# Attention into a two-layer feed-forward on one core: the last product of the attention as column tiles

## The chip, the cores and the metric

One core of one Trainium2 chip runs the whole program. The metric is the device time of one execution in microseconds, as a median of several runs. The engines are named as in the profile: PE (matrix product), PEld (its weight loads), DVE, ACT, POOL, and SP, which issues the transfers.

## What is computed

Four batches of eight heads, 576 positions, 64 numbers per head. The attention has no softmax: both `q` and `k` go through a feature map of 256 features, and the sums over the positions are taken before `q` comes in.

```python
def phi(x):
    proj = np.einsum('bhsd,df->bhsf', x, w_phi)
    proj = proj - np.max(np.abs(proj), axis=-1, keepdims=True)
    return np.concatenate([np.exp(proj), np.exp(-proj)], axis=-1)
q_p, k_p = (phi(q), phi(k))
kv = np.einsum('bhsf,bhsd->bhfd', k_p, v)
z = np.sum(k_p, axis=2)
num = np.einsum('bhsf,bhfd->bhsd', q_p, kv)
den = np.einsum('bhsf,bhf->bhs', q_p, z)[..., None] + 1e-06
x = num / den
```

The result, as 2304 tokens of 512 numbers, goes through `g = h * cos(h)`, `h = x @ w_in`, `g @ w_out` and then through a second layer with the square of the positive part in place of `h * cos(h)`. Both layers have 2048 hidden numbers.

## The kernel before

The attention works in 16 units; a unit `u` is two heads of one batch. Its steps carry short names. `PJk`, `PJq`, `PJt` (lines 512 and 521) are the projections on PE: two heads lie in the two row halves of the array. `R...` takes the maximum and subtracts it on DVE, `E...` and `QE...` are the exponentials on ACT, `Q...` (lines 574 and 571) are transposes on PE, `V0`, `V1`, `Vt` (lines 546 and 554) build `kv` and, in a 65th column, `z` in a bank of PSUM.

The steps that the change touches come last. `KS` and `KZ` (lines 564 and 566, DVE) copy `kv` of both heads into `ks`, four blocks of 64 columns: numerators of head 0, the column `z` of head 0 sixty-four times, `z` of head 1 sixty-four times, numerators of head 1. `N` (line 593) multiplies: for one head and one half of the positions (288 columns), two matmuls, one for each half of the 256 features, each with a weight of 128 columns, 64 of numerators and 64 that all give the denominator. There are four such steps per unit, `N00`, `N10`, `N01`, `N11`, each into a PSUM bank of its own, of which there are two. `C` (line 601, ACT) copies each to `tm`. `D1` (SP) brings the 576 denominators of each head from one partition into `cp`, 32 partitions of 36; `I` (DVE) adds 1e-6 and inverts; `D3` writes them to DRAM, `D4` reads them back, spread over 64 partitions per head, and `Z0`, `Z1` (line 631, POOL) multiply, one head each, into `xbuf`, from which the feed-forward reads.

Data is 32-bit float. A 32-bit float matmul of the program is two PE instructions in the trace, with a weight load for each; a transpose, and a matmul of the feed-forward (declared float32r), is one.

The order on each engine is fixed ahead: the tables `STEPS`, `W_STEPS` and `F_STEPS` give each step an engine, a planned cost and a place, and `arrange` lists the steps as they can start by those costs. Between the steps of the units stand the preparation of the feed-forward's weights (`wload`, `wa` to `lo`, on SP, ACT, DVE and POOL) and the first four blocks of the feed-forward. After that the feed-forward follows in a plain loop, three matmuls for each product (lines 289 to 291 and 385).

Of the kernel before, what the change touches and what calls it, by code (L numbers as in the profile page):

```python
# [8 lines left out]
F32 = mybir.dt.float32  # L9
# [24 lines left out]
    "PJk": ("PE", 1.2, -0.0861),  # L34
    "PJq": ("PE", 1.0, -1000.0),
    "PJt": ("PE", 0.5, -0.531),
    "Rk0": ("DVE", 1.39, -0.7547),
    "Rk1": ("DVE", 1.39, -0.587),
    "Rq0": ("DVE", 1.39, 0.0807),
    "Rq1": ("DVE", 1.39, 1.743),  # L40
    "Rt": ("DVE", 0.86, -0.2191),
    "Ek0": ("ACT", 1.12, -2.3061),
    "Ek1": ("ACT", 1.12, -0.6222),
    "Et": ("ACT", 0.52, 0.2442),
    "V0": ("PE", 1.8, -0.4006),
    "V1": ("PE", 1.8, 0.3704),
    "Vt": ("PE", 0.46, 0.8122),
    "KS": ("DVE", 0.44, 0.23),
    "KZ": ("DVE", 0.44, -0.9258),
    "Q0": ("PE", 0.45, 0.6667),  # L50
    "Q1": ("PE", 0.45, 0.8333),
    "Qt": ("PE", 0.12, -1.179),
    "QE0": ("ACT", 1.1, 0.5433),
    "QE1": ("ACT", 1.1, 0.8521),
    "QEt": ("ACT", 0.5, -1.2755),
    "N00": ("PE", 0.98, 1.1469),
    "N10": ("PE", 0.98, 1.4122),
    "N01": ("PE", 0.98, 0.8229),
    "N11": ("PE", 0.98, 1.4454),
    "C00": ("ACT", 0.42, 0.8958),  # L60
    "C10": ("ACT", 0.42, 1.1975),
    "C01": ("ACT", 0.42, 0.8069),
    "C11": ("ACT", 0.42, 2.6994),
    "D1": ("SP", 0.75, 1.3),
    "I": ("DVE", 1.2, 1.7326),
    "D3": ("SP", 0.32, 1.5),
    "D4": ("SP", 1.1, 1.6),
    "Z0": ("POOL", 1.5, 1.9905),
    "Z1": ("POOL", 1.5, 0.312),
# [5 lines left out]
    "wa": ("ACT", 0.58, 15.5),  # L75
    "wb": ("ACT", 0.58, -0.631),
    "wc": ("ACT", 0.58, 0.629),
    "j0": ("DVE", 0.75, -8.494),
    "j1": ("DVE", 1.0, 6.091),
    "add": ("POOL", 1.32, 29.772),  # L80
    "mul": ("POOL", 1.32, -17.661),
    "hi": ("ACT", 0.56, 14.013),
    "lo": ("POOL", 1.32, 41.761),
# [4 lines left out]
    "xh": ("ACT", 0.56, 23.758),  # L88
    "xl": ("DVE", 0.69, 3.914),
    "G1": ("PE", 2.73, 8.892),  # L90
    "A1": ("ACT", 1.05, -24.304),
    "A2a": ("DVE", 0.7, -3.676),
    "A2b": ("DVE", 0.9, 41.064),
    "B1": ("ACT", 1.15, 36.696),
    "B2": ("DVE", 0.7, -14.68),
    "B3": ("ACT", 0.55, 23.9),
    "B4": ("DVE", 0.69, 22.441),
# [61 lines left out]
def attention_ffn_kernel(  # L159
# [27 lines left out]
    with tc.manual_schedule():  # L187
# [281 lines left out]
        with ExitStack() as actx:  # L469
# [31 lines left out]
            def rows(h):  # L501
                return slice(D * h, D * (h + 1))
# [56 lines left out]
            def KS(u, part):  # L559

                kv = kv_t[u]
# [25 lines left out]
            SH = S // 2  # L587

            def N(u, h, half):
# [8 lines left out]
            def C(u, h, half):  # L598
                if h == half == 0:
                    tm_t[u] = late("tm", [P, 2, S])  # L600
                nc.scalar.activation(
                    out=tm_t[u][:, h, half * SH:(half + 1) * SH], in_=nm_t.pop((u, h, half))[:, 0:SH], func=ACTF.Copy
                )
# [14 lines left out]
            def D3(u):  # L618
                db = db_t[u] = dp.tile([2, S], F32, tag="db", name="db", bufs=2)
                nc.sync.dma_start(out=db.rearrange("h (a b) -> (h a) b", a=NI), in_=cp_t.pop(u))  # L620
# [7 lines left out]
            def Z(u, h):  # L628
                b, hp = UNITS[u]
                r = rows(h)  # L630
# [15 lines left out]
            for u in range(NU):  # L646
# [18 lines left out]
                st("KS", (KS, u, 0), ("Vt",), [("ks",)], [("kv",)])  # L665
                st("KZ", (KS, u, 1), ("Vt", "KS"), (), [("kv",), ("ks",)])
# [6 lines left out]
                before = ()  # L673
                for half in range(2):
                    for h in range(2):
                        n, tiles = f"{h}{half}", [("nm", h, half)]
# [7 lines left out]
                for h in range(2):  # L684
                    st(f"Z{h}", (Z, u, h), ("D4",), (), [("tm",), ("dn",)])
# [120 lines left out]
```

## Time and profile before

| | us |
|---|---|
| median of 3 runs | 988.17 (988.00 to 988.29) |
| the profiled execution | 988.67 |
| its span, first to last instruction | 986.9 |
| PE busy within the span | 977.4 (99%) |
| last product, line 593, PE busy | 70.9, 256 instructions |
| same, its weight loads on PEld | 45.1 |
| copies of line 601 on ACT | 25.1, 64 instructions |
| multiplications of line 631 on POOL | 45.6, 32 instructions |

The attention takes the first 190 us or so of the span, the rest is the feed-forward. A busy PE row is not the time that a matmul costs: a matmul's shown length includes the way through the array, so the next one starts well before it ends. The chain of work that ended last shows for each piece the time until the next piece starts, and so what the piece costs.

### The profile page before, as it was taken

The page shows a single profiled execution, that of the slowest core. Times are in us where ns is not written, and L with a number is a line of the kernel's source. Part 1 is how long each engine was busy: PE and PEld are TensorE (multiplying, and loading weights), DVE is VectorE, ACT ScalarE, POOL GpSimd, SP SyncE. Part 2 cuts the span into 40 slices and gives each one's busy share as a digit, 9 for nine tenths or more (in the row PEclk, how much of TensorE's full clock was granted, in tenths as well). Part 3 has the DMA queues.
Part 4 walks back from the last instruction along what each step waited for, and adds up shares of the span by engine and source line. Part 5 has one row for each costly group of instructions (what it writes and reads, how often), then busy time and mean ns, then how long its engine had stood idle before and what let it go on. Part 6 is the DMA issues. An engine that isn't in the chain of part 4 may idle for free.

```text
span 986.9 us, 14043 instructions
## 1 busy us (share of the span) xinstructions
PE 977.4 (99%) x5305; PEld 831.9 (84%) x5305; DVE 548.8 (56%) x944; ACT 625.6 (63%) x1213; POOL 123.3 (12%) x98
## 2 busy tenths in 40 slices
PE   9999999999999999999999999999999999999998
PEld 8988899888889888888888888888888888888897
DVE  5788887789966655565458888983112111211211
ACT  5888888698967665575559879995333433433343
POOL 1577686501000000000000000000000000000000
PEclk9999999999999999999999999999999999999999
DMA  6566532152000000000036660001000000100010
GB/s 228 182 201 225 190 114 88 38 192 77 1 1 2 1 1 1 1 0 1 1 90 193 196 192 12 1 1 44 1 1 17 27 1 1 43 1 1 1 44 22
DMA packets 23284, 60.01 MB, mean 61 GB/s; under 512 B 4400, under 2 KB 4528, under 8 KB 23216
## 3 DMA queue, kind: packets, MB, share of 16 engines
q1 hardware_dynamic: 23072, 59.04, 18.4%
q8 instruction: 42, 0.69, 0.3%
q14 instruction: 26, 0.21, 0.1%
q10 hardware_dynamic: 144, 0.07, 0.0%
HBM read 54.23 MB, written 4.79 MB: 60 GB/s over the span
## 4 chain that ended last, share of the span: by engine, by line
PE 85%; DVE 5%; ACT 4%; DMA 2%; issue 2%; POOL 1%; SPq 0%; DVEq 0%; POOLq 0%
PE acc L385 36%; PE h L291 12%; PE h L290 12%; PE h L289 12%; PE nm L593 4%; PE kv L546 4%; PE pj L512 2%; PE tp L574 1%; DVE tr L311 1%; DMA db<-cp 1%; DMA dn<-db 1%; ACT tr L305 1%; DVE w L259 1%; ACT tr L304 1%; DVE mag L246 1%
## 5 line engine op out<-in xcount | busy, mean ns | idle before, releaser
L327 DVE TENSOR_TENSOR g<-tr,g 128x512 fp32r<-128x512 f32 (+1 forms) x160 | 101.8, 636 | 275.0 <-ACT g L324 274.0
L289 PE MATMUL h<-xs,w 128*128 128x512 f32 (+1 forms) x640 | 235.8, 369 | 0.0
L291 PE MATMUL h<-xs,w 128*128 128x512 f32 (+1 forms) x640 | 235.5, 368 | 0.0
L290 PE MATMUL h<-xs,w 128*128 128x512 f32 (+1 forms) x640 | 235.4, 368 | 0.0
L385 PE MATMUL acc<-g,w 128*128 128x512 f32 (+1 forms) x960 | 208.4, 368 | 0.8 <-DVE g L327 0.8
L385 PE MATMUL acc<-w,g 128*128 128x512 f32 x864 | 206.8, 389 | 0.0
L385 PEld LDWEIGHTS acc<-g,w 128*128 128x128 f32 x960 | 168.1, 189 | 31.5 <-DVE g L327 1.7
L385 PEld LDWEIGHTS acc<-w,g 128*128 128x128 f32 x864 | 161.4, 188 | 32.9
L324 ACT ACTIVATE g<-tr 128x512 fp32r<-128x512 f32 (+1 forms) x160 | 93.8, 586 | 128.0 <-PE acc L385 94.5
L289 PEld LDWEIGHTS h<-xs,w 128*128 128x128 f32 x640 | 120.7, 189 | 20.6
L290 PEld LDWEIGHTS h<-xs,w 128*128 128x128 f32 x640 | 120.6, 188 | 20.5
L291 PEld LDWEIGHTS h<-xs,w 128*128 128x128 f32 x640 | 120.7, 189 | 20.0
L307 ACT ACTIVATE tr<-h 128x512 f32<-128x512 f32 (+1 forms) x80 | 44.2, 552 | 103.8 <-PE h L291 102.7
L309 DVE SCALAR_TENSOR_TENSOR tr<-tr,h 128x512 f32<-128x512 f32 (+1 forms) x80 | 50.7, 634 | 63.1 <-ACT tr L305 61.8
L319 DVE SCALAR_TENSOR_TENSOR tr<-tr,h 128x512 f32<-128x512 f32 (+1 forms) x80 | 50.6, 633 | 40.4 <-ACT tr L315 39.8
L593 PE MATMUL nm<-eq,ks 128*128 128x288 f32 x256 | 70.9, 410 | 0.4 <-DVE ks L566 0.4
L314 ACT ACTIVATE tr<-tr 128x512 f32<-128x512 f32 (+1 forms) x80 | 46.8, 585 | 26.7 <-DVE tr L311 26.7
L304 ACT ACTIVATE tr<-h 128x512 f32<-128x512 f32 (+1 forms) x80 | 43.6, 545 | 30.0 <-PE h L291 29.7
L546 PEld LDWEIGHTS kv<-v,e 128*128 128x128 f32 x512 | 59.8, 192 | 1.7
L546 PE MATMUL kv<-v,e 128*128 128x65 f32 x512 | 59.0, 273 | 0.0
L527 DVE TENSOR_REDUCE m<-pj 128x4 f32<-128x512 f32 (+1 forms) x80 | 49.4, 617 | 8.2 <-PE pj L512 8.2
L631 POOL TENSOR_TENSOR xbuf<-tm,dn 64x576 f32<-64x576 f32 x32 | 45.6, 1426 | 62.4 <-DMA dn<-db 61.2
(55 smaller groups left out, 1052.5 us busy)
## 6 DMA issues: line engine op xcount, KB each, us to landing
raw<-in_dram SPq DMA_DIRECT2D x64, 512.0 KB, 4.3
kq<-in_dram SPq DMA_DIRECT2D x16, 384.0 KB, 3.4
v<-in_dram SPq DMA_DIRECT2D x16, 330.0 KB, 4.3
dn<-db SPq DMA_DIRECT2D x32, 144.0 KB, 3.1
out_dram<-ot SPq DMA_DIRECT2D x18, 256.0 KB, 3.1
kq<-in_dram SPq DMA_DIRECT2D x16, 256.0 KB, 3.5
cp<-tm SPq DMA_DIRECT2D x32, 2.2 KB, 2.4
db<-cp SPq DMA_DIRECT2D x16, 4.5 KB, 3.8
```

The lines of the kernel that those rows point to most:

```text
L289: nc.tensor.matmul(out=hps, lhsT=ih[:, kk, :], rhs=xh, start=kk == 0, stop=False)
L290: nc.tensor.matmul(out=hps, lhsT=ih[:, kk, :], rhs=xl, start=False, stop=False)
L291: nc.tensor.matmul(out=hps, lhsT=il[:, kk, :], rhs=xh, start=False, stop=kk == KDM - 1)
L304: nc.scalar.activation(out=t, in_=h_t[c], func=ACTF.Copy, scale=INV_2PI, bias=ROUND)
L309: nc.vector.scalar_tensor_tensor(out=r, in0=t, scalar=-C1, in1=h_t[c], op0=ALU.mult, op1=ALU.add)
L319: nc.vector.scalar_tensor_tensor(out=t, in0=r, scalar=1.0, in1=h_t.pop(c), op0=ALU.subtract, op1=ALU.mult, reverse0=True)
L324: nc.scalar.activation(out=g[:, 0], in_=t, func=ACTF.Copy)
L327: nc.vector.tensor_tensor(out=g[:, 1], in0=t, in1=f(g[:, 0]), op=ALU.subtract)
L385: nc.tensor.matmul(out=o, lhsT=l, rhs=r, start=c == 0 and i == 0, stop=c == KFF - 1 and i == 2)
L527: nc.vector.tensor_reduce(out=m[:, 0:n], in_=pj[:, 0:n, :], axis=AX.X, op=ALU.max, apply_absolute_value=True)
L546: nc.tensor.matmul(out=acc[:, s, h, 0:D + 1], lhsT=e[:, t, s, :], rhs=v_t[u][:, t, h, 0:D + 1], start=t == 0 and h == 0 and s == 0, stop=F ...
L593: nc.tensor.matmul(out=nm[:, 0:SH], lhsT=ks_t[u][:, s, 2 * h:2 * h + 2, :].rearrange("p a d -> p (a d)"), rhs=eq_t[u][:, h, s, half * SH:( ...
```

## The change

`ks` now has only numerators and one column `z` for each head, and is copied in one instruction. `N` is one step for a unit. It takes both PSUM banks, one for each half of the positions. First come eight matmuls of 288 columns with weights of 64 columns: head 0 writes partitions 0 to 63 of the bank, head 1 partitions 64 to 127 (tiles of 128 rows by 64 columns of the array). Then sixteen matmuls of 144 columns, whose weight is one column `z` thirty-two times: each of four strips of 32 partitions takes one head and one quarter of the positions (tiles of 128 by 32), into columns 288 to 431 of the same bank. `C` copies 432 columns, twice a unit. `D1` reads four partitions, 32 apart, for each half; `D3` is two transfers; `Z` is one multiplication over 128 partitions. All places in the tables are new, so the order on the engines is too; the planned costs change only for the steps touched (`N` 3.5, `C` 0.5, `D3` 0.75).

```diff
-    "N00": ("PE", 0.98, 1.1469),
...
-    "C00": ("ACT", 0.42, 0.8958),
...
+    "N": ("PE", 3.5, 1.6213),
+    "C0": ("ACT", 0.5, 0.9339),
+    "C1": ("ACT", 0.5, 0.1895),
...
-                if part == 0:
-                    ks = ks_t[u] = own("ks", [P, 2, 4, D])
-                    nc.vector.tensor_copy(ks[:, :, 0:4:3, :], kv[:, :, :, 0:D])
-                else:
-                    nc.vector.tensor_copy(ks_t[u][:, :, 1:3, :], kv[:, :, :, D:D + 1].to_broadcast([P, 2, 2, D]))
+                ks = ks_t[u] = own("ks", [P, 2, 2, D + 2])
+                nc.vector.tensor_copy(ks[:, :, :, 0:D + 1], kv_t.pop(u)[:, :, :, 0:D + 1])
...
-                nm = nm_t[u, h, half] = bank("nm")
-                for s in range(2):
-                    nc.tensor.matmul(
-                        out=nm[:, 0:SH], lhsT=ks_t[u][:, s, 2 * h:2 * h + 2, :].rearrange("p a d -> p (a d)"),
-                        rhs=eq_t[u][:, h, s, half * SH:(half + 1) * SH], start=s == 0, stop=s == 1,
-                    )
+                for half in range(2):
+                    nm_t[u, half] = bank("nm")
+                for half in range(2):
+                    for s in range(2):
+                        for h in range(2):
+                            nc.tensor.matmul(
+                                out=nm_t[u, half][rows(h), 0:SH], lhsT=ks[:, s, h, 0:D], rhs=eq[:, h, s, half * SH:(half + 1) * SH],
+                                start=s == 0, stop=s == 1,
+                            )
+                for half in range(2):
+                    for s in range(2):
+                        for i in range(4):
+                            h, o = i // 2, half * SH + (i % 2) * SQ
+                            nc.tensor.matmul(
+                                out=nm_t[u, half][32 * i:32 * i + 32, SH:SH + SQ], lhsT=ks[:, s, h, D:D + 1].to_broadcast([P, 32]),
+                                rhs=eq[:, h, s, o:o + SQ], start=s == 0, stop=s == 1, skip_group_check=True,
+                            )
...
-                for h in range(2):
-                    nc.sync.dma_start(out=cp[h * NI:(h + 1) * NI, :], in_=tm_t[u][D - D * h:D - D * h + 1, h, :])
+                for half in range(2):
+                    nc.sync.dma_start(out=cp[half * NI:(half + 1) * NI, :], in_=tm_t[u][0:P:32, half, SH:SH + SQ])
...
-                nc.sync.dma_start(out=db.rearrange("h (a b) -> (h a) b", a=NI), in_=cp_t.pop(u))
+                for half in range(2):
+                    nc.sync.dma_start(out=db[:, half * SH:(half + 1) * SH], in_=cp[half * NI:(half + 1) * NI, :])
...
-                    out=xbuf[r, hp, b * S:(b + 1) * S], in0=tm_t[u][r, h, :], in1=dn_t[u][r, :], op=ALU.mult
+                    out=xbuf[:, hp, b * S:(b + 1) * S].rearrange("p (a n) -> p a n", a=2), in0=tm_t.pop(u)[:, :, 0:SH],
+                    in1=dn_t.pop(u).rearrange("p (a n) -> p a n", a=2), op=ALU.mult,
...
+                st("N", (N, u), ("KS", "QE0", "QE1", "QEt"), [("nm", 0), ("nm", 1)], [("ks",), ("eq",)])
+                st("C0", (C, u, 0), ("N",), [("tm",)], [("nm", 0)])
+                st("C1", (C, u, 1), ("N", "C0"), (), [("nm", 1)])
```

The order on PE through one unit in the middle of the attention, before (`nm` is the last product, `kv` the sums, `tp` transposes, `pj` projections; the `x` at the end counts matmuls of the program):

```order
L593 MATMUL nm<-eq,ks 128x288 x2
L546 MATMUL kv<-v,e 128x65 x16
L593 MATMUL nm<-eq,ks 128x288 x4
L574 MATMUL tp<-ident,pq 128x128 x4
L554 MATMUL kv<-v,et 128x2x65 x2
L512 MATMUL pj<-wph,kq 128x128 x8
L512 MATMUL pj<-wph,kq_1137 128x128 x8
L574 MATMUL tp<-ident,pq 128x128 x4
L593 MATMUL nm<-eq,ks 128x288 x2
L521 MATMUL pj<-wph,kq_1137 128x128 x2
L571 MATMUL tp<-ident,pt 128x128
```

And the same engine through one unit of the changed kernel:

```order
L562 MATMUL tp<-ident,pq 128x128 x4
L585 MATMUL nm<-eq,ks 64x288 x8
L593 MATMUL nm<-eq,ks 32x144 x16
L539 MATMUL kv<-v,e 128x65 x8
L562 MATMUL tp<-ident,pq 128x128 x4
L514 MATMUL pj<-wph,kq_1452 128x128 x2
L539 MATMUL kv<-v,e 128x65 x8
L559 MATMUL tp<-ident,pt 128x128
L505 MATMUL pj<-wph,kq 128x128 x8
L505 MATMUL pj<-wph,kq_1548 128x128 x8
L547 MATMUL kv<-v,et 128x2x65 x2
```

The four pieces of the last product are now one block of two kinds of tiles, between a transpose and the next unit's `kv`; the two projections and the `kv` sums are otherwise the same work.

On SP, which issues the transfers, one unit in the middle of the attention before (`cp`, `db` and `dn` carry the denominators, `raw` is a feed-forward weight, `kq` and `v` are a unit's inputs):

```order
L620 DMA db<-cp 32x36
L625 DMA dn<-db 64x576 x2
L219 DMA raw<-in_dram 128x1024
L611 DMA cp<-tm 16x1x36 x2
L219 DMA raw<-in_dram 128x1024
L487 DMA kq<-in_dram 128x512
L488 DMA kq_1137<-in_dram 128x768
L489 DMA v<-in_dram 128x660
```

And in the changed kernel:

```order
L620 DMA db<-cp 2x8x36 x2
L625 DMA dn<-db 64x576 x2
L212 DMA raw<-in_dram 128x1024
L609 DMA cp<-tm 16x1x36 x2
L480 DMA kq<-in_dram 128x512
L481 DMA kq_1238<-in_dram 128x768
L482 DMA v<-in_dram 128x660
L212 DMA raw<-in_dram 128x1024
```

What moved there is little: the write of `db` is two transfers, still directly ahead of the read of `dn`.

## Rows read from the trace of the kernel before

**Rows 1.** The page: busy time of each engine; the clock by slices.
```profile
PE 977.4 (99%) x5305; PEld 831.9 (84%) x5305; DVE 548.8 (56%) x944; ACT 625.6 (63%) x1213; POOL 123.3 (12%) x98
PEclk9999999999999999999999999999999999999999
```

**Rows 2.** Stretches: length, busy us (instructions) per engine, clock, DMA share, GB/s.
```profile
0.00:20.00 20.00, 17.71 (x151) 15.77 (x151) 12.61 (x22) 9.13 (x19) 0.70 (x6) 1.00 0.64 215
...
40.00:60.00 20.00, 18.68 (x148) 16.61 (x147) 16.15 (x29) 16.91 (x40) 15.43 (x12) 1.00 0.72 232
...
80.00:100.00 20.00, 19.82 (x167) 17.15 (x167) 16.56 (x29) 17.77 (x39) 16.07 (x13) 1.00 0.65 211
...
120.00:140.00 20.00, 20.00 (x169) 18.07 (x166) 17.30 (x31) 17.73 (x40) 16.42 (x13) 1.00 0.41 125
...
260.00:987.00 727.00, 722.28 (x3453) 608.77 (x3452) 340.66 (x581) 414.70 (x770) 0.00 (x0) 1.00 0.10 30
```

**Rows 3.** Chain that ended last, one unit: start, us to next piece, what.
```profile
100.13 0.97 PE nm L593 x4
101.10 3.52 PE kv L546 x32
104.62 2.00 PE nm L593 x8
106.61 0.44 PE tp L574 x4
107.05 0.45 PE kv L554 x4
107.50 1.99 PE pj L512 x32
109.48 0.59 PE tp L574 x4
110.07 0.97 PE nm L593 x4
111.04 0.44 PE pj L521 x4
111.48 0.11 PE tp L571
111.59 0.97 PE nm L593 x4
```

**Rows 4.** The same chain earlier, where it leaves PE.
```profile
30.69 4.94 DMA db<-cp
...
36.20 3.48 DMA dn<-db
...
41.30 1.42 POOL xbuf L631
...
53.44 0.97 PE nm L593 x4
...
60.98 3.61 DMA raw<-in_dram
...
88.66 0.97 PE nm L593 x4
```

**Rows 5.** Timeline: start, us, eight weight loads and eight matmuls of line 593.
```profile
104.40 1.76 PEld L593 LDWEIGHTS nm<-eq,ks 128*128 128x128 f32 x8
104.45 2.16 PE L593 MATMUL nm<-eq,ks 128*128 128x288 f32 x8
```

**Rows 6.** Groups by line and shape: busy us, mean ns of one | idle before.
```profile
L601 ACT ACTIVATE tm<-nm 128x288 f32<-128x288 f32 x64 | 25.1, 416 | 12.0 <-PE nm L593 7.8 <-POOL xbuf L631 3.3 <-issue 0.6
L585 ACT ACTIVATE eq<-tp 128x512 f32<-128x512 f32 x64 | 34.7, 595 | 17.4 <-PE tp L574 17.0
L566 DVE COPY ks<-kv 128x256 f32<-128x256 f32 x16 | 6.6, 412 | 0.0
L631 POOL TENSOR_TENSOR xbuf<-tm,dn 64x576 f32<-64x576 f32 x32 | 45.6, 1426 | 62.4 <-DMA dn<-db 61.2
L249 POOL TENSOR_TENSOR mag<-mag,raw 128x512 f32<-128x512 f32 x20 | 26.3, 1313 | 1.6
```

More of the change, by code (lines that the diff above doesn't have):

```diff
@@ L33 @@
     "load": ("SP", 1.5, -1.2),
[L34 removed]
+    "PJk": ("PE", 1.2, -0.956),
     "PJq": ("PE", 1.0, -1000.0),
[L36 to L55, printed above, removed]
[L56 to L63 removed]
+    "PJt": ("PE", 0.5, 0.1833),
+    "Rk0": ("DVE", 1.39, -1.2383),
+    "Rk1": ("DVE", 1.39, -0.0484),
+    "Rq0": ("DVE", 1.39, 0.4179),
+    "Rq1": ("DVE", 1.39, 0.7208),
+    "Rt": ("DVE", 0.86, 0.2315),
+    "Ek0": ("ACT", 1.12, 0.6024),
+    "Ek1": ("ACT", 1.12, -0.6443),
+    "Et": ("ACT", 0.52, -2.1609),
+    "V0": ("PE", 1.8, -2.4809),
+    "V1": ("PE", 1.8, 1.0348),
+    "Vt": ("PE", 0.46, 0.094),
+    "KS": ("DVE", 0.44, 0.387),
+    "Q0": ("PE", 0.45, 0.3741),
+    "Q1": ("PE", 0.45, 1.0206),
+    "Qt": ("PE", 0.12, 0.4218),
+    "QE0": ("ACT", 1.1, -1.2185),
+    "QE1": ("ACT", 1.1, 1.4953),
+    "QEt": ("ACT", 0.5, 2.3738),
+    "N": ("PE", 3.5, 1.6213),
+    "C0": ("ACT", 0.5, 0.9339),
+    "C1": ("ACT", 0.5, 0.1895),
     "D1": ("SP", 0.75, 1.3),
[L65 to L66 removed]
+    "I": ("DVE", 1.2, 0.3695),
+    "D3": ("SP", 0.75, 1.5),
     "D4": ("SP", 1.1, 1.6),
[L68 to L69 removed]
+    "Z": ("POOL", 1.5, 0.4143),
 }
@@ L74 @@
     "wload": ("SP", 0.42, -8.0),
[L75 to L83, printed above, removed]
+    "wa": ("ACT", 0.58, 8.047),
+    "wb": ("ACT", 0.58, -14.026),
+    "wc": ("ACT", 0.58, -1.16),
+    "j0": ("DVE", 0.75, 5.723),
+    "j1": ("DVE", 1.0, -31.34),
+    "add": ("POOL", 1.32, 19.558),
+    "mul": ("POOL", 1.32, -29.025),
+    "hi": ("ACT", 0.56, 10.49),
+    "lo": ("POOL", 1.32, 7.455),
 }
@@ L87 @@
 F_STEPS = {
[L88 to L97, printed above, removed]
+    "xh": ("ACT", 0.56, 41.17),
+    "xl": ("DVE", 0.69, 11.019),
+    "G1": ("PE", 2.73, 10.528),
+    "A1": ("ACT", 1.05, 2.19),
+    "A2a": ("DVE", 0.7, -16.948),
+    "A2b": ("DVE", 0.9, -14.477),
+    "B1": ("ACT", 1.15, -1.164),
+    "B2": ("DVE", 0.7, 20.764),
+    "B3": ("ACT", 0.55, 37.626),
+    "B4": ("DVE", 0.69, -14.05),
 }
@@ L672, in attention_ffn_kernel @@
                 st("QEt", (QE, u, "t"), ("Qt", "QE0"), (), [("tp", 2)])
[L673 to L676, printed above, removed]
-                        st("N" + n, (N, u, h, half), ("KZ", f"QE{h}", *before, *(("QEt",) if half else ())), tiles, [("ks",), ("eq",)])
-                        st("C" + n, (C, u, h, half), ("N" + n, *("C" + b[1:] for b in before)), [] if before else [("tm",)], tiles)
-                        before = ("N" + n,)
-                st("D1", (D1, u), ("C01", "C11"), [("cp",)], [("tm",)])
+                st("N", (N, u), ("KS", "QE0", "QE1", "QEt"), [("nm", 0), ("nm", 1)], [("ks",), ("eq",)])
+                st("C0", (C, u, 0), ("N",), [("tm",)], [("nm", 0)])
+                st("C1", (C, u, 1), ("N", "C0"), (), [("nm", 1)])
+                st("D1", (D1, u), ("C1",), [("cp",)], [("tm",)])
                 st("I", (I, u), ("D1",), (), [("cp",)])
@@ L683, in attention_ffn_kernel @@
                 st("D4", (D4, u), ("D3",), [("dn",)], [("db",)])
-                for h in range(2):
-                    st(f"Z{h}", (Z, u, h), ("D4",), (), [("tm",), ("dn",)])
+                st("Z", (Z, u), ("D4",), (), [("tm",), ("dn",)])
             for n in range(NEARLY - 1):
@@ L723, in attention_ffn_kernel @@
             keys = arrange(steps)
-            behind = max(i for i, key in enumerate(keys) if key[0] in STEPS and key[0] not in ("C01", "C11", "D1", "I", "D3", "D4", "Z0", "Z1"))
+            behind = max(i for i, key in enumerate(keys) if key[0] in STEPS and key[0] not in ("C0", "C1", "D1", "I", "D3", "D4", "Z"))
             def emit(keys):
```

31 lines of the change are left out of this document (14 added, 17 removed).

## The prediction

> **What bounds the kernel now.** I read the busy times first. PE is busy for 977.4 of 986.9 us [rows 1], so only what shortens PE's own work, or a wait of PE, can shorten the whole. The stretches show where PE is not full: it lacks 2.29 us of the first 20, 1.32 in 40:60 and 0.18 in 80:100, and nothing in 120:140, while ACT and DVE stand there at 17.7 and 17.3 of 20 us [rows 2]. From 260 us on the feed-forward runs at 722.28 of 727 us, and the change leaves its matmuls alone. The clock is granted in full in every stretch [rows 1, 2], the higher of its two levels (2.4 GHz), so no term below is a matter of the clock. What is at stake is the attention, some 190 us.
>
> Next comes the chain that ended last. From one first piece of the last product (100.13) to the next like it (111.59) every piece is PE, and its start-to-start times are the cost of a unit: 11.46 us. The last product has 0.97 + 0.97 + 2.00 = **3.94 us** of that [rows 3], 16 units make 63 us. But earlier the chain leaves PE: between 30.7 and 53.4 us it goes through the denominators' transfers and POOL, and so again between 61.0 and 88.7 [rows 4]. There PE is nearly full, yet others set the pace.
>
> **Numerators.** Eight matmuls of 288 columns as before, so sixteen PE instructions; four cost 0.97 us, one 0.243 [rows 3]. If the two column halves of the array work side by side, that is 8 rounds of 0.243 = 1.94 us; if not, 3.88. No column tile is in this trace; its nearest row is the projection, with two heads in the two row halves. It has 32 instructions in 1.99 us, whereas four instructions with weights and data of the same 128 columns on the whole array cost 0.44 (line 521), 0.11 each: one after the other, 32 would cost 3.52 [rows 3]. After 0.20 us for going in (next but one paragraph), 16 pairs share 1.79 us, 0.112 a pair, as much as one alone. So row halves overlap fully, though the program issues both instructions of head 0 ahead of those of head 1. I take the same for columns: **1.94 us**.
>
> **Denominators.** Sixteen matmuls, so 32 instructions, of 144 columns: 0.243 / 2 = 0.121, by the small surplus of shorter instructions 0.125. Before, this work was free, since it filled the second half of a full weight. Four strips side by side make 8 rounds, **1.00 us**; two at a time 1.95 to 2.00; one at a time 4.0. I take four, by the projection's row, which lies nearest and shows no loss at two; nothing here shows four.
>
> **Going from one kind of tile to another.** Entering the projections: 1.99 us less 16 x 0.112 is 0.20 us. Leaving: the four transposes behind them cost 0.59 us, four others 0.44, so 0.15 [rows 3]. The new block has three such changes (whole array to halves, to strips, back to whole), 0.20 + 0.20 + 0.15 = 0.55. Part of this is a first weight load that nothing covers, and the loads of 64 and 32 columns are smaller, so I take **0.50 us**; the bounds are 0 (column tiles need no change) and 0.60. Sum of `N`: 1.94 + 1.00 + 0.50 = **3.44 us**, 0.50 less than 3.94, over 16 units **8.0 us**.
>
> **The weight loads** become 48 for a unit instead of 16, but narrower. Eight loads lie between 104.40 and 106.16, the eight matmuls of the same rows of the array between 104.45 and 106.61 [rows 5]: loads go on under running matmuls, and I cost them at nothing. The Trainium skill ("TensorE: Matmul & The Clock Gate", Part 3, The mechanism) says that a load overlaps a running matmul only when it aims at other rows of the array; column tiles share all rows, so the page speaks against this change. These rows disagree with it for whole-array loads. What it would cost is rival 2.
>
> **Other engines.** ACT copies 32 x 432 columns instead of 64 x 288: 416 ns at 288 and 595 at 512 give 0.80 ns a column and 0.53 us for 432, so 1.06 instead of 1.66 us a unit. DVE loses one copy of `ks`, 0.41 us a unit. POOL multiplies once over 128 partitions; a multiplication costs by its columns (64x576 takes 1426 ns, 128x512 takes 1313), so 1.4 us a unit go [rows 6]. All of this lies beside PE and gains nothing in units like that of rows 3; it is cover for the shorter period. SP issues one more `db` transfer a unit ahead of the `dn` reads; behind these stand weight and unit loads. Bounds: nothing, or up to 4.94 us later for one unit's `Z` [rows 4], for which only the first feed-forward block waits, far later. I take nothing.
>
> **The waits.** `N` now waits for `KS` and all three `QE` at once, and all of PE queues behind it, the next unit's `kv` first. In the new order the `ks` that a block reads is that of the unit before: a whole round of `kv` stands between its `KS` and the block, so the block itself should not wait. The `KS` that does run then, 0.41 us on DVE [rows 6], has the block's 3.4 us as cover before the next `kv` needs the bank that it empties; without that cover it would cost some 0.4 us a unit. `C0` can start only when its bank has the last strip, some 3 us after the block's beginning instead of 1; behind it on ACT stand exponentials. Both banks are taken, but the next block is a period away. Cost: nothing, at most 0.4 us a unit.
>
> **What of the gain is lost.** The 8.0 us are saved only where PE sets the pace. The two stretches off PE in the chain make 22.7 + 27.7 = 50.4 us [rows 4], 4.4 units, at most 2.2 us of the gain; the first two units, in the 20 us that wait for inputs [rows 2], at most 1.0 more. There the chain itself gets shorter by one POOL multiplication a unit, so not all is lost: between 0 and 3.2, I take **2.0**. Result: 6.0 us less. The span becomes 986.9 - 6.0 = 980.9, the profiled execution 988.67 - 6.0 = 982.7, and as that lies 0.5 above the median of 988.17, **982.2 us**. Its own range: `N` between 3.05 and 3.65 and 0 to 3.2 lost, 976 to 987.
>
> **Rivals.** 1: four strips overlap only two at a time. `N` = 1.94 + 1.95 + 0.50 = 4.39, 0.45 more than before, 7.2 us slower: **995.4**. For it: no row shows four at once; against it, that two halves lose nothing. It decides against the change from the point where a round of four costs 0.19 instead of 0.125 us. The Trainium skill (same page, Part 3, Measured speedup vs the span model) gives 2.38 for three column tiles, 0.79 of full overlap; an estimate from that page would put `N` at 4.2 and the time near 992. Rows 3 show 3.52 / 1.79 = 1.97 of 2 for rows, so I keep full overlap.
>
> 2: weight loads are not covered in column tiles. A 128-column load takes at least 0.11 us (line 554 costs that per instruction whatever its 130 columns need [rows 3]), so 0.056 for 64 and 0.028 for 32 columns; a round of either kind has 0.11 us of loads, 16 rounds 1.8 us. `N` = 5.2, 1.3 us x 16 = 21 us slower: **1009**. The page named above would have it so; rows 5 are against it.
>
> 3: the change doesn't do what it says, and tiles run one after the other: 3.88 + 4.0 + 0.5 = 8.4, 4.4 x 16 = 71 us slower: **1059**. The projections speak against it.
>
> 4: another engine takes over. ACT and DVE are at 17.7 and 17.3 of 20 us in 120:140 [rows 2]; in a period of 10.96 instead of 11.46 they would stand at 18.5 and 18.1 even without their savings of 0.6 and 0.41 us a unit, so they fit, but the order is new and each wait of 0.4 us a unit eats the rest. Then 0 to 2 us are gained: **987.5**.
>
> 5: changing tiles costs nothing. `N` = 2.94, 16 us less 3 lost: **975**.
>
> **How the numbers follow.** Chances: forecast 0.64, rival 1 0.09, rival 2 0.06, rival 3 0.03, rival 4 0.11, rival 5 0.07. A measurement of this kernel tells 0.2% (2.0 us) from no change. Faster: the forecast and rival 5, 0.71. Same: rival 4, 0.11. Slower: rivals 1 to 3, 0.18. The range leaves out the slower ones (0.18) and little else: 975 to 990.
>
> **What would show it.** In the changed trace the chain through one unit should have the two rows of `N` at 2.1 to 2.2 us (halves, with their entry) and 1.2 us (strips, with theirs), and the instruction behind them some 0.15 late; a period near 11.0; the last `kv` of the attention some 5 us earlier. A strips row of 2.0 us is rival 1, loads that stand between matmuls instead of under them rival 2, rows of 3.9 and 4.0 rival 3. PE idle by 0.4 us a unit before `N` or `kv`, released by ACT or DVE, is rival 4. I am wrong in the sum if the strips' round is not near 0.125 us, and wrong in the loss if PE idles in 20:100 for more than some 3 us.

## The result: 978.2 us, 10 us less, and the profile after

The changed kernel takes 978.20 us as a median, the kernel before 988.29 beside it; the ratio is 0.9895, with an interval of 0.9879 to 0.9910. A second series gave 978.46 against 989.53 (0.9889, 0.9874 to 0.9903). The forecast was 982.2 with a range of 975 to 990: sign and range were right, but 4 us of the gain were missed. One execution of the first series ran at a granted clock of 0.16 from about 420 us on and is left out; the profile of after is from the second series (profiled execution 978.45, span 976.7).

The page of the changed kernel, busy time of each engine and the clock by slices, to be held against [rows 1]:

```profile
PE 969.0 (99%) x5817; PEld 815.2 (83%) x5817; DVE 540.7 (55%) x928; ACT 617.9 (63%) x1181; POOL 101.4 (10%) x82
PEclk9999999999999999999999999999999999999999
```

PE is still the engine that is nearly always busy, the clock is granted in full throughout, and POOL has 22 us less to do. The chain that ended last through one unit of the changed kernel (start, us to the next piece, what), which answers to [rows 3]:

```profile
101.60 2.09 PE nm L585 x16
103.69 1.12 PE nm L593 x32
104.81 0.64 PE kv L547 x4
...
105.89 0.45 PE pj L514 x4
106.33 1.73 PE kv L539 x16
...
109.92 1.99 PE pj L505 x32
111.90 0.64 PE kv L547 x4
...
112.98 2.09 PE nm L585 x16
```

The halves cost 2.09 us, the strips 1.12. The piece behind them (line 547) costs 0.64; it was 0.45 before, in another place [rows 3], and four such instructions of line 514 still cost 0.45, so 0.19 goes to leaving the strips. The 0.64 at 111.90 is the same effect behind the projections. **`N` costs 2.09 + 1.12 + 0.19 = 3.40 us** against 3.94 before. That is 0.54 x 16 = 8.6 us.

The first feed-forward matmul starts at 180.34 us instead of 190.51, 10.17 earlier; the last matmul starts at 972.45 instead of 982.66, 10.21 earlier. So the whole gain is there when the feed-forward begins, and 1.6 us of it is not `N`. (Of the last unit, the changed kernel has the whole `N` behind that first matmul, the kernel of before only three of its four pieces; the leg from there to the last matmul is 792.1 us in both.) The stretches 0:200 in twenties, summed, of the kernel before and then of the changed kernel (busy us of each engine):

```profile
sum 200.00, PE 195.07 PEld 173.39 DVE 153.71 ACT 155.28 POOL 120.32; mean PE 19.51 PEld 17.34 DVE 15.37 ACT 15.53 POOL 12.03
```

```profile
sum 200.00, PE 196.69 PEld 165.07 DVE 152.50 ACT 157.22 POOL 98.23; mean PE 19.67 PEld 16.51 DVE 15.25 ACT 15.72 POOL 9.82
```

PE lacks 4.93 us before and 3.31 after: 1.62 us less waiting, with 8.6 the 10.2 that were found. What PE waited for in 0:200, of before and then of after (engine, line, releaser: us in total, times, longest), shows which waits went:

```profile
PE nm L499 <- DVE eq L493: 1.6, 1, 1.6
PE tp L574 <- ACT eq L585: 1.3, 2, 0.7
PE pj L521 <- DVE pk L529: 0.9, 2, 0.7
PE tp L571 <- ACT eq L585: 0.8, 1, 0.8
PE nm L593 <- DVE ks L566: 0.4, 1, 0.4
```

```profile
PE nm L492 <- DVE eq L486: 1.6, 1, 1.6
PE pj L514 <- DVE pk L522: 0.9, 2, 0.7
PE tp L559 <- ACT eq L573: 0.4, 1, 0.4
PE tp L562 <- ACT eq L573: 0.3, 1, 0.3
```

Transposes waited 2.1 us for exponentials on ACT, now 0.7; the wait of `N` for `ks` (0.4) is gone. The wait of 1.6 at the very start is the same in both. The 1.6 us that were won are a balance: waits of 2.6 us went, 1.5 of them between 50 and 88 us and 1.1 at 188 to 190 us, in the last unit; new waits of 1.0 us came, nearly all between 15 and 23 us, in the first units.

### The profile page after: what moved, and what is told of

It is laid out like the page before. It is cut to its first block, busy times and chain, and to the rows that moved or that the text cites. A ratio compares the mean times of both kernels' runs of the same rounds, so it can differ in the third digit from the quotient of the medians.

```text
span 3653.6 us, 15041 instructions
## 1 busy us (share of the span) xinstructions
PE 3644.8 (100%) x5817; PEld 2622.1 (72%) x5817; DVE 543.1 (15%) x928; ACT 620.6 (17%) x1181; POOL 100.9 (3%) x82
## 4 chain that ended last, share of the span: by engine, by line
PE 97%; DVE 1%; ACT 1%; DMA 0%; issue 0%; POOL 0%; SPq 0%; DVEq 0%; POOLq 0%
PE acc L378 47%; PE h L282 15%; PE h L283 15%; PE h L284 15%; PE kv L539 1%; PE nm L585 1%; PE pj L505 1%; PE nm L593 0%; PE tp L562 0%; DMA raw<-in_dram 0%; DVE tr L304 0%; ACT tr L298 0%; PE kv L547 0%; DVE mag L239 0%; DVE w L252 0%
## 5 line engine op out<-in xcount | busy, mean ns | idle before, releaser
L378 PE MATMUL acc<-w,g 128*128 128x512 f32 x864 | 1166.7, 1694 | 0.0
L378 PEld LDWEIGHTS acc<-w,g 128*128 128x128 f32 x864 | 785.8, 914 | 342.1 <-issue 342.1
L283 PE MATMUL h<-xs,w 128*128 128x512 f32 (+1 forms) x640 | 764.2, 1194 | 0.0
L282 PE MATMUL h<-xs,w 128*128 128x512 f32 (+1 forms) x640 | 763.7, 1193 | 0.0
L284 PE MATMUL h<-xs,w 128*128 128x512 f32 (+1 forms) x640 | 762.6, 1192 | 0.0
L378 PE MATMUL acc<-g,w 128*128 128x512 f32 (+1 forms) x960 | 630.9, 886 | 0.6 <-DVE g L320 0.6
L378 PEld LDWEIGHTS acc<-g,w 128*128 128x128 f32 x960 | 443.4, 475 | 171.3 <-issue 154.8
L282 PEld LDWEIGHTS h<-xs,w 128*128 128x128 f32 x640 | 434.4, 679 | 161.5 <-issue 156.0
L283 PEld LDWEIGHTS h<-xs,w 128*128 128x128 f32 x640 | 434.3, 679 | 161.4 <-issue 155.8
L284 PEld LDWEIGHTS h<-xs,w 128*128 128x128 f32 x640 | 435.5, 680 | 155.9 <-issue 150.2
L304 DVE SCALAR_TENSOR_TENSOR tr<-tr 128x512 f32<-128x512 f32 (+1 forms) x80 | 50.9, 636 | 2.1
L307 ACT ACTIVATE tr<-tr 128x512 f32<-128x512 f32 (+1 forms) x80 | 46.5, 582 | 24.2 <-DVE tr L304 24.1
L298 ACT ACTIVATE tr<-tr 128x512 f32<-128x512 f32 (+1 forms) x80 | 47.1, 589 | 2.6
```

What stands on the lines that cost most here:

```text
L282: nc.tensor.matmul(out=hps, lhsT=ih[:, kk, :], rhs=xh, start=kk == 0, stop=False)
L283: nc.tensor.matmul(out=hps, lhsT=ih[:, kk, :], rhs=xl, start=False, stop=False)
L284: nc.tensor.matmul(out=hps, lhsT=il[:, kk, :], rhs=xh, start=False, stop=kk == KDM - 1)
L298: nc.scalar.activation(out=t, in_=t, func=ACTF.Copy, bias=-ROUND)
L304: nc.vector.scalar_tensor_tensor(out=r, in0=t, scalar=-C2, in1=r, op0=ALU.mult, op1=ALU.add)
L378: nc.tensor.matmul(out=o, lhsT=l, rhs=r, start=c == 0 and i == 0, stop=c == KFF - 1 and i == 2)
```

## Experiments

Every kernel below is the changed kernel with one edit, but for one that is the kernel before with the new places. Times are medians, with the kernel before that ran beside them.

| edit | us | before | ratio, interval |
|---|---|---|---|
| none (the change again) | 978.46 | 989.53 | 0.9889, 0.9874 to 0.9903 |
| halves and strips in turns | 982.96 | 989.53 | 0.9933, 0.9916 to 0.9949 |
| strips computed twice | 994.12 | 989.53 | 1.0045, 1.0030 to 1.0060 |
| half of the strips left out | 979.34 | 989.15 | 0.9893, 0.9873 to 0.9913 |
| head 0, then head 1 | 994.62 | 989.15 | 1.0047, 1.0030 to 1.0065 |
| strips one after the other | 1003.04 | 989.97 | 1.0136, 1.0121 to 1.0151 |
| new product, places of before | 1013.78 | 989.53 | 1.0238, 1.0200 to 1.0276 |
| product of before, new places | 1001.92 | 989.15 | 1.0124, 1.0100 to 1.0148 |
| `Z` as two instructions | 987.51 | 989.15 | 0.9979, 0.9962 to 0.9997 |
| `C` as four instructions | 978.58 | 989.97 | 0.9893, 0.9878 to 0.9907 |
| projections next to the block | 982.47 | 989.97 | 0.9929, 0.9912 to 0.9945 |

### The change again: where did the gain arise

> The changed kernel once more, for a trace that runs at full clock to the end. Theory: 978.2 us as measured; in the attention the halves' row at 2.09 us and the strips' at 1.12 us a unit, and the feed-forward, whose matmuls are unchanged, as long as before, so that all of the 10.1 us lie ahead of its first matmul. Rival: some 1 to 1.5 us of them come out of the feed-forward's first block, where the leftovers of the attention's last units stand among its steps; then the distance between the first feed-forward matmul and the end is shorter than before by that.

Measured: 978.46 us. The two starts named above settle it: 10.17 us are there when the feed-forward begins and 10.21 at its end. The rival, a gain inside the feed-forward, is out.

### Halves and strips in turns: what a change of tiles costs

```diff
                 for half in range(2):
                     for s in range(2):
                         for h in range(2):
...
-                for half in range(2):
                     for s in range(2):
                         for i in range(4):
```

> Each half of the positions gets its numerators and then its strips at once, so the block goes halves, strips, halves, strips: two more changes of tile for a unit, the same matmuls. Theory: a change of tile costs 0.14 to 0.15 us on PE and PE sets the pace, 0.29 x 16 = 4.6 us slower than the changed kernel, 982.8. Rival: what looks like the price of a change is the first uncovered load at the block's edge only, and the first copy starts earlier, then no slower than 978.2.

Measured: 982.96 us, 4.5 more than the change alone, as expected. The block in the chain (the strips are line 592 there):

```profile
103.42 1.12 PE nm L585 x8
104.54 0.63 PE nm L592 x16
...
```

The second pair, left out here, reads the same. Two of these pairs cost 3.50 us where one block cost 3.21: 0.29 for two more changes of tiles, **0.14 each**; 0.29 x 16 = 4.6 us. A change of tiles is a real cost, and PE sets the pace closely enough that all of it shows.

### The strips twice: do four run at once

```diff
-                for half in range(2):
+                for half in (0, 0, 1, 1):
                     for s in range(2):
                         for i in range(4):
```

> The sixteen strip matmuls of a unit are done twice, with the same result. Theory: four strips run side by side at 0.122 us a round and PE has no slack: 8 rounds x 0.1225 = 0.98 us a unit, 15.7 us slower, 993.9. Rival: 1.5 to 3 us of that vanish in waits of PE that the new order has anyway, 991 to 992. If the strips really overlapped only two at a time, 31 us slower, 1009.

Measured: 994.12 us, 15.7 more. The row of the doubled strips:

```profile
110.64 2.10 PE nm L593 x64
```

32 more instructions cost 2.10 - 1.12 = 0.98 us; 8 rounds of four at 0.1225. Rival 1 (two at a time) would need 1.95. That 0.98 x 16 = 15.7 us appear whole in the time says again that PE sets the pace in all units.

### Half of the strips: does PE still set the pace if `N` gets shorter

This kernel leaves out one half of the features in the denominators, to see what a shorter `N` would bring.

```diff
-                    for s in range(2):
+                    for s in (1,):
                         for i in range(4):
...
-                                rhs=eq[:, h, s, o:o + SQ], start=s == 0, stop=s == 1, skip_group_check=True,
+                                rhs=eq[:, h, s, o:o + SQ], start=True, stop=True, skip_group_check=True,
```

> Leaves out the strips of the first half of the features, so the denominators lack a part: eight strip matmuls a unit instead of sixteen. Theory: PE still sets the pace, 4 rounds x 0.1225 = 0.49 us a unit, 7.8 us faster than the changed kernel, 970.6. Rival: ACT and DVE, at 17 to 18.5 of 20 us, take over below a period of 11 us; then only 0 to 4 us, 974 to 978.

Measured: 979.34 us, no gain at all and outside both expectations, though the strips' row fell from 1.12 to 0.63 us (0.49 x 16 = 7.8 us). The chain around 60 us shows where it went:

```profile
55.72 1.39 POOL xbuf L630
57.10 1.24 POOL mag L239
...
58.43 1.30 POOL mag L242
...
59.75 0.63 ACT w L248
...
61.91 1.04 ACT e L531 x2
...
62.99 1.77 PE kv L539 x14
...
66.25 3.31 PE kv L539 x16
...
69.78 2.93 PE pj L505 x32
```

PE waited once for 2.2 us for an exponential (`e`), which stood on ACT behind a step of the weights that waited for POOL; POOL's multiplication ahead of it had itself waited 1.8 us for a transfer. After the wait the granted clock fell, 0.83 in the stretch 60:80 and 0.50 from 66 to 70 us: sixteen `kv` instructions cost 3.31 us instead of 1.73, the projections 2.93 instead of 1.99, so PE ran at the lower of its two levels (1.2 GHz) for a while. The wait and the clock make 2.2 and about 3.4 us (an estimate, 0.17 x 20) of the 8.7 between the theory and the measured time; the rest is not placed. Elsewhere PE kept the shorter period: from 73.78 to 84.23 us a unit took 10.45 (10.94 - 0.49). So the theory that PE alone sets the pace holds down to the changed kernel's period and not everywhere below it: at this one place the other engines have no room.

### Head 0 and then head 1, and the strips one after the other: who finds the free tile

Nothing is computed differently here, only the order of the matmuls within the block.

```diff
-                for half in range(2):
-                    for s in range(2):
-                        for h in range(2):
+                for h in range(2):
+                    for half in range(2):
+                        for s in range(2):
                             nc.tensor.matmul(
                                 out=nm_t[u, half][rows(h), 0:SH], ...
```

> The numerators in another order of issue: all eight PE instructions of head 0, then all eight of head 1 (before, they took turns by two). Theory: each column tile has a queue that is filled far enough ahead, the halves overlap as before, 978.4. Rival: PE looks ahead only by a few instructions; then head 1 starts late, up to 16 x 0.243 = 3.88 instead of 1.94 us a unit, up to 31 us slower, 1009; between the two, the trace shows how far it looks.

Measured: 994.62 us, 16.2 more, between the two expectations. The halves' row in the chain:

```profile
108.56 3.11 PE nm L585 x16
```

3.11 - 2.09 = 1.02, x 16 = 16.3 us. The stretches of this block, line 585 alone (length, PE busy and instructions, PEld busy and instructions, clock, DMA share, GB/s; an instruction that reaches over a border counts on both sides):

```profile
108.45:109.50 1.05, 1.01 (x4) 0.60 (x5) 1.00 0.41 79
109.50:110.53 1.03, 1.03 (x9) 0.72 (x8) 1.00 0.92 310
110.53:111.60 1.07, 1.07 (x6) 0.41 (x3) 1.00 0.79 246
```

Head 0's first four instructions run alone; head 1's first starts at 109.521, together with head 0's fifth (109.515), though head 1's tile had been free from the start; then both go side by side, and four of head 1 are left alone at the end. Twelve rounds of 0.2425 us instead of eight. An instruction overtakes three that wait for a busy tile, and not more. (The trace does not name the tile: it is read from the order in the program, and from the first instruction of each tile, shown 457 ns long where the others have 406.) That the fifth is also the first into the other bank is not the reason: in the changed kernel the strips overtake one another within one bank, four first instructions within 19 ns (103.621 to 103.640 us).

The same for the strips:

```diff
-                for half in range(2):
-                    for s in range(2):
-                        for i in range(4):
+                for i in range(4):
+                    for half in range(2):
+                        for s in range(2):
                             h, o = i // 2, half * SH + (i % 2) * SQ
```

> The changed kernel with the strips outermost: the four products of strip 0 stand together, then those of strip 1, 2 and 3 (the halves stay in turns). Same products, same loads. Theory (TensorE looks only about four products with their loads ahead for one that another part of the array can take): a strip has four products, eight instructions, so the next strip starts only when the strip before is about half done, and 32 instructions go in some 20 rounds instead of 8; at 0.12 us a round 1.4 us more per unit x 16 = 22 us, 995 to 1003. Rival (it was the distance of eight of the halves that was too far, and four are within reach): 978.4 to 980.

Measured: 1003.04 us, 24.6 more than the change, at the upper end of the theory. The strips' row in the chain:

```profile
102.37 2.65 PE nm L593 x32
```

2.65 - 1.12 = 1.53 us more a unit, 24.5 in 16. Again the next strip's first instruction starts with the fifth of the strip before (102.815 and 102.821); with each strip starting four late, 32 instructions need 4 + 12 + 4 = 20 rounds instead of 8, and at 0.1225 us the 12 more cost 1.47. The side-by-side work hangs on the order in which the program names the tiles: taking turns from one matmul to the next is what makes it happen. The changed kernel's own order needs just this reach: the first instruction of its fourth strip overtakes the second ones of three strips.

### New product in the old places, old product in the new places

One takes the tables of numbers from before for every step that both have (`N`, `C`, `KS` and `Z` at the places of one of the steps that they replace), the other gives the product of before the new tables.

```diff
-    "PJk": ("PE", 1.2, -0.956),
+    "PJk": ("PE", 1.2, -0.0861),
...
-    "PJt": ("PE", 0.5, 0.1833),
+    "PJt": ("PE", 0.5, -0.531),
...
```

> The changed kernel with the places of the tables from the kernel before (N where N00 stood, C0 and C1 where C10 and C11 stood, Z where Z0 stood); the planned costs stay. It tells the new product from the new order. Theory: the new product alone gives 8.6 us and the order is worth little: 978 to 981. Rival: the old order makes the one large block wait for the last of its three exponentials in each unit, since it now needs all at once; 0.5 to 1 us a unit are lost, 986 to 994.

Measured: 1013.78 us, far outside both expectations: the new product in the order of before is 24 us slower than the kernel before. PE's waits in 0:215 and the worst stretch:

```profile
PE tp L559 <- ACT eq L573: 2.5, 7, 0.4
PE kv L539 <- ACT e L531: 2.3, 12, 0.2
```

```profile
20.00:40.00 20.00, 19.24 (x174) 13.39 (x177) 9.96 (x20) 12.57 (x26) 8.92 (x7) 0.78 0.53 168
```

The waits are short (none over 0.7 us but the one of 1.6 at the start) and many. All of PE's waits there sum to 9.0 us, 5.8 more than in the changed kernel. The clock adds to that: 0.78 in 20:40, 0.91 in the two stretches behind, 0.92 over 0:200, some 16 us (an estimate, 0.08 x 200). In the chain the halves cost 4.04 us in 20:40 instead of 2.09. Waits and clock do not place all of the 35 us between this kernel and the changed one.

> The product of the kernel before with the places of the changed kernel's tables (the four N at the place of N, C00 and C10 at that of C0, C01 and C11 at that of C1, both Z at that of Z, KZ at that of KS). It tells how much of the gain is the order alone. Theory: the new order belongs to the new block and is worth nothing to the old product, 988 to 996. Rival: the 1.6 us that PE idles less in the changed kernel are the order's, and come here too, 986.5 to 987.

Measured: 1001.92 us, 12.8 above the kernel before and outside both expectations. PE waits there for `ks` (2.5 and 2.0 us) and for the exponentials of `eq` (2.7). So neither half of the change is worth anything alone, as far as one mapping of the places for each can show: the new order loses 13 us without the new product, the new product loses 24 without the new order, and both together gain 10.

### `Z` as two instructions again: is POOL's saving needed

```diff
-                nc.gpsimd.tensor_tensor(
-                    out=xbuf[:, hp, b * S:(b + 1) * S].rearrange("p (a n) -> p a n", a=2), in0=tm_t.pop(u)[:, :, 0:SH],
-                    in1=dn_t.pop(u).rearrange("p (a n) -> p a n", a=2), op=ALU.mult,
-                )
+                tm, dn = tm_t.pop(u), dn_t.pop(u)
+                for h in range(2):
+                    r = rows(h)
+                    nc.gpsimd.tensor_tensor(
+                        out=xbuf[r, hp, b * S:(b + 1) * S].rearrange("p (a n) -> p a n", a=2), in0=tm[r, :, 0:SH],
+                        in1=dn[r, :].rearrange("p (a n) -> p a n", a=2), op=ALU.mult,
+                    )
```

> The multiplication on POOL in two instructions of 64 partitions, as before the change, 1.4 us a unit more on POOL. Theory: POOL has that room, no change, 978.4. Rival: POOL's multiplications stand in the round trip of the denominators that sets the pace in 30:90, so what POOL saved there is part of the gain, 979.5 to 981.5.

Measured: 987.51 us (984.41 to 990.66 over seven runs): **some 9 of the 10 us are gone**, with PE's instructions unchanged. Both expectations were far too low. The chain in the stretch 52 to 66:

```profile
55.99 1.49 POOL xbuf L633
...
57.55 1.36 POOL mag L239
...
58.98 1.30 POOL mag L242
...
60.31 0.63 ACT w L248
60.94 0.97 ACT eq L573 x2
...
62.35 1.16 ACT e L531 x2
...
63.56 2.32 PE kv L539 x14
```

and what waited there, with the stretches of PE that follow:

```profile
ACT w L248 <- POOL mag L242: 3.7, 1, 3.7
PE kv L539 <- ACT e L531: 1.7, 1, 1.7
```

```profile
60.00:80.00 20.00, 18.26 (x202) 15.97 (x199) 13.77 (x26) 17.46 (x36) 13.78 (x12) 0.91 0.60 188
...
120.00:140.00 20.00, 19.44 (x202) 17.34 (x203) 17.61 (x28) 16.74 (x36) 16.50 (x13) 0.91 0.29 94
```

POOL's 1.4 us more a unit make a step of the feed-forward's weights late (`mag`, two steps on POOL); ACT stands 3.7 us at line 248 and waits for it (2.2 us at the same place in the changed kernel), with two exponentials of `q` and two of `k` behind it in its fixed order; PE's sums wait 1.7 us for those (0.1 in the changed kernel), and then the granted clock falls to 0.91 over 20 us.

At 120 us PE waits again, 0.7 us, and the clock is 0.91 in 120:140, but the way there is another. ACT waits for DVE, and DVE is late because of instructions that stand while POOL works (start, us, what, idle time before it):

```profile
112.40 2.97 POOL L633 TENSOR_TENSOR xbuf<-tm,dn 64x576 f32<-64x576 f32 x2 [0.28 <-DMA dn<-db]
...
114.01 1.39 DVE L613 TENSOR_SCALAR cp<-cp 32x36 f32<-32x36 f32 x1
...
119.80 0.63 ACT L531 ACTIVATE e<-pk 128x512 f32<-128x512 f32 x1 [2.15 <-DVE pk L522]
```

The small addition of `I` (line 613) ends 0.03 us behind POOL's second multiplication (115.40 and 115.37 us). Of its 16 in this kernel, the ten that started while POOL was at work took 0.27 to 1.39 us and ended 30 to 38 ns behind POOL's instruction; the other six took 0.16. In all they take 9.4 us on DVE, 7.3 in the changed kernel. Two steps of the weights behind the one shown (lines 235 and 237) take 1.27 and 1.40 us in the same way, where most of their kind take 0.42. So PE, which has nothing to do with `Z`, pays for it by way of ACT at 60 us, and by way of DVE and ACT at 120.

### `C` as four instructions: is ACT's saving needed

```diff
-                nc.scalar.activation(out=tm_t[u][:, half, :], in_=nm_t.pop((u, half))[:, 0:SH + SQ], func=ACTF.Copy)
+                nm = nm_t.pop((u, half))
+                for c in (slice(0, SH), slice(SH, SH + SQ)):
+                    nc.scalar.activation(out=tm_t[u][:, half, c], in_=nm[:, c], func=ACTF.Copy)
```

> The changed kernel with each copy of a tile on ScalarE as two (288 and 144 columns) instead of one of 432: by the rows of the changed kernel a copy of 432 columns takes 0.524 us; the nearest rows (0.37 to 0.41 us at 256 columns, 0.27 to 0.31 at 128) make the two about 0.71, so ScalarE gets 0.19 x 2 = 0.38 us per unit back of the 0.6 that the change saves on it. TensorE's instructions stay as they are. Theory (ScalarE's saving is cover in the same way as GpSimd's, since the exponentials of the next units stand behind the copies): 2 to 6 us longer than the changed kernel, 980.5 to 984.5, with waits of the sums (line 539) for exponentials. Rival (ScalarE has room in its period, only GpSimd's chain was short of it): 978.0 to 979.0.

Measured: 978.58 us, no change of the median; the rival was right. The two pieces of a copy take 409 and 295 ns instead of one of 524, 0.36 us a unit back on ACT. The room is narrow: the slowest of the four executions, which is the profiled one, took 980.45, and PE waits there 0.6 us for an exponential of `k` (line 539) and 0.6 for one of `q` (line 559) that it hardly waits for in the changed kernel. ACT, at 63% of the span, has room for 0.36 us a unit; POOL, at 10%, has none for 1.4: the cover is a matter of the chain and not of how busy an engine is on average. But the two amounts differ, and that the whole 0.6 us of ACT's saving, or 1.4 us on ACT, would be free is not shown.

### The projections next to the block: a better version?

```diff
-            keys = arrange(steps)
+            keys = arrange(steps)
+            pe = [k for k in keys if steps[k][0] == "PE"]
+            for a in range(len(pe) - 4):
+                if [k[0] for k in pe[a:a + 2]] == ["PJk", "PJq"] and pe[a + 4][0] == "N":
+                    at = keys.index(pe[a])
+                    for k in pe[a + 2:a + 4]:
...
+                        keys.remove(k)
+                        keys.insert(at, k)
+                        at += 1
```

> The changed kernel with one thing moved on TensorE: where the steps PJk, PJq, Vt and Q stand ahead of the block in this order, Vt and Q go ahead of the projections, so that the projections (row tiles of 64) stand directly before the block (column tiles of 64) and TensorE changes its tiling straight from the one to the other, instead of going back to the full array for Vt and Q between them. This removes one change of tiling in each unit where it applies, some 12 of 16. Theory (a change of tiling costs 0.14 to 0.20 us wherever it stands): 12 x 0.14 to 0.20 = 1.7 to 2.4 us less, 976.0 to 976.8. Rival (Vt and Q come too early for the exponentials and subtractions that they wait for, or the projections too late for those behind them): 980 to 984, with waits in those rows.

Measured: 982.47 us, 4.0 more than the change, as the rival had it. It applied in 7 units, not 12, and there PE went from row tiles to column tiles in 0.20 us from start to start, as long as from the whole array to columns: one change instead of two. But PE's waits in 0:200 grew:

```profile
PE tp L562 <- ACT eq L573: 3.6, 6, 1.0
```

Transposes wait 3.6 us instead of 0.3, since ACT has not yet emptied the bank that they write. Moving two steps by 2 us on PE costs more than the changes of tiles that it saves. This version does not beat the changed kernel.

## Why the prediction was right, and where it was short

**Numerators: right.** The two halves' instructions start 6 to 7 ns apart, a pair every 0.2425 us; 8 rounds make the 1.94 that were taken from 0.97 / 4. (The prediction worked the 0.112 us of a pair of projections and the 0.20 for going in out of one another; the trace of before has a pair every 0.112 us, so both stand.)

**Denominators: right.** Four strips start 6 to 7 ns apart, a round every 0.1225 us instead of 0.125; 8 rounds are 0.98. Rival 1 and rival 3 fall. The jump from rows (two tiles, seen) to columns (four, not seen) held, but only because the program takes turns between the tiles from one matmul to the next; the two kernels with another order lost 1.0 and 1.5 us a unit. The prediction saw the overtaking in the projections' row and did not ask how far it reaches. The Trainium skill ("TensorE: Matmul & The Clock Gate", Part 3, The mechanism) says that matmuls stay strictly in the program's order; this trace disagrees, since of four strips, each two instructions long, the last strip's first starts 19 ns after the first strip's first, before that strip's second, which is issued ahead of it. The page's 2.38 for three column tiles is not seen here either; two halves and four strips overlap in full.

**Changes of tiles: right.** `N` is 3.40 us, its rounds are 1.94 + 0.98, so three changes cost 0.48 where 0.50 was taken: 0.14 for one between halves and strips (the kernel that takes turns), 0.19 for leaving, the rest for entering. Rival 5, changes for nothing, falls.

**Weight loads: right.** The timeline's loads under the block of the changed kernel:

```profile
101.53 1.65 PEld L585 LDWEIGHTS nm<-eq,ks 128*64 128x64 f32 x16 [0.17 <-issue]
103.62 0.89 PEld L593 LDWEIGHTS nm<-eq,ks 128*32 128x32 f32 x32 [0.44 <-issue]
```

They lie under the matmuls of the same lines (101.53 to 103.69 and on to 104.81), and the rounds are no longer than the columns make them by [rows 3]. All tiles of this block share all 128 rows, and 48 loads a unit cost nothing that can be seen, so rival 2 falls. The Trainium skill's rule (same page and part) that a load overlaps only a matmul on other rows is not borne out by these rows. The same section also lets a load into a background weight buffer go ahead of running matmuls; these rows would fit that, and the prediction left it out.

**What of the gain is lost: this step failed.** It stood at 2.0 us lost (0 to 3.2), because in [rows 4] the chain leaves PE from 30.7 to 53.4 us and from 61.0 to 88.7, which was read as others setting the pace there. In fact 1.6 us were won on top. In those 50.4 us PE stood still for 1.5 us only, in the kernel before. The changed kernel's chain in the first of those stretches:

```profile
35.95 2.09 PE nm L585 x16
38.04 1.12 PE nm L593 x32
...
46.89 2.09 PE nm L585 x16
```

It is PE up to 52.9 us, with a period of 10.94: the transfers of the denominators and POOL no longer end last there. (From 52.9 to 61.6 us it leaves PE once more, by a weight's transfer, and PE waits 0.1 us at its end.) New waits in the first units came as allowed for, 1.0 us; what the prediction did not see is that waits of 2.6 us would go. What made them go is not told apart. Before the 1.5 us that lay between 50 and 88 us the chain of [rows 4] passes POOL's multiplication, so POOL's shorter work is a candidate; the 1.1 us in the last unit stood behind transposes, ACT and `ks`, with no POOL in the chain from 185 us on. Of the savings beside PE, POOL's is the one that the new kernel is shown to need: giving its second multiplication back costs 9 us, giving 0.36 us of ACT's back costs nothing in the median. 8.6 + 1.6 is 10.2; 8.0 - 2.0 was 6.0.

**Other engines: right in the sum, with no price on the cover.** The prediction took the savings beside PE as cover for the shorter period and as nothing in the sum. Cover is what POOL's is, but it carries nearly the whole gain. POOL stood at 16.42 of 20 us in 120:140 [rows 2], next to the ACT and DVE figures from which rival 4 was worked out. Rival 4 was the right question, asked of two engines and not of the third. Nor was the price of such a wait seen: 0.4 us a unit were allowed for, when one wait of 1.7 us was followed by a lower clock as well.

**Waits: right.** `N` waits for nothing in 0:200 of the changed kernel, and the next `kv` does not wait for its bank. DVE's 16 copies of `ks` are hidden. The chain's period is 10.94 us from 35.95 to 46.89 and 11.38 from 101.60 to 112.98; over the seven units from 35.95 to 112.98 its mean is 77.03 / 7 = 11.0, the forecast.

**One bound of the range was off.** The range of the forecast itself began at 976; an `N` of 3.05 us with nothing lost is 0.89 x 16 = 14.2 us less, which is 974. The measured time lies above both.

What stays open: the profiled span of the kernel with two `Z` is 9.0 us longer than that of the change. The first feed-forward matmul starts 7.2 us later (187.52 instead of 180.34), and the leg behind it is 1.9 us longer. Of the 7.2, PE's waits explain 2.8 (6.0 us in 0:200 instead of 3.2) and the two stretches at 0.91 about 3.6 (an estimate, 0.09 x 40); of the 1.9, waits for DVE behind 187 us explain 1.3 (1.8 instead of 0.5). The rest is not placed. Whether the order of the steps or POOL's shorter work has the larger part in the 1.6 us that were won is open too: the new product in the old order loses too much elsewhere to show it.

## What to carry to other kernels

Work that fills only some columns or rows of the array can be put side by side and then costs one tile's time, but the tiles must take turns matmul by matmul, and each change of tiling cost 0.14 to 0.20 us here, so tiles of one shape belong together. Before a saving on an engine off the critical path is written down as nothing, follow the order on that engine to the next step that the bound engine waits for: 1.4 us a unit of POOL was worth 9 us here, 0.36 us of ACT nothing in the median. A chain that leaves the bound engine does not say that others set its pace: look at how long the engine stood still there. An order made for one product is not neutral for another; neither half of this change could have been judged alone.

## What the hardware showed that was not expected

- An instruction of PE overtakes three that wait for a busy tile, and no more: both orders in blocks of eight let the second tile start with the fifth instruction of the first. 3.11 and 2.65 us instead of 2.09 and 1.12.
- Waits of PE of 0.7, 1.7 and 2.2 us in a busy stretch were followed by a lower granted clock (0.91, 0.91 and 0.83 over 20 us), and the rows behind them cost up to twice as much (3.31 instead of 1.73). Others were not: in the product of before with new places waits of 1.3 and 1.4 us, at 81 and 92 us, left the clock at 1.00. A kernel with many short waits (none over 0.7 us after the start) fell to 0.78 over 20 us.
- Where DVE's small addition on `cp` started while POOL was at work, it ended some 30 ns or more behind POOL's instruction (30 to 38 ns in the kernel with two `Z`, 32 to 139 in the changed one), and took up to 1.39 us instead of 0.16. That makes a second way from POOL's work to PE.
- A change of tiles costs 0.14 us between halves and strips and 0.19 from the strips to the whole array, and going from row tiles straight to column tiles costs no more than from the whole array (0.20 us from start to start in both).
